# Decode attention at the DMA limit: wo rows as one packet a partition, 112 V tokens in column groups, and the last V piece cut by partitions

## The chip, the cores and the metric

The kernel runs on one core of a Trainium2 chip. The metric is device time in microseconds (us); lower is better. The span is the stretch that the profile covers, from the first to the last instruction; it is about 2 us shorter than the time.

## The reference, cut to what matters

```python
# D = 448; 16 query heads, 8 KV heads (two query heads each), 65,536 keys, head size 256, bf16
q = (x @ wq) ...                                  # one token
scores = einsum("bhqd,bhkd->bhqk", q, k) * 256**-0.5
o = einsum("bhqk,bhkd->bhqd", softmax(scores), v)
a = o.reshape(1, 1, 16 * 256) @ wo                # wo: 4096 x 448
b = ...                                           # a small token mixer, hidden behind the loads
return g * a + (1 - g) * b                        # g: sigmoid gate
```

One token attends to 65,536 keys in each of 8 KV heads. K and V are 268 MB each and are read once. A "pair" below is one KV head with its two query heads. DVE is VectorE, HBM the memory from which K, V and wo are read (544.22 MB by the page). A packet is one entry of the trace's DMA records, here mostly one partition's run (65,536 bytes, 128 tokens, in a whole block); a piece has landed when the trace records the last completion on its semaphore.

## The kernel before

K and V come in 32 blocks of 8 MB each: partition p holds 128 tokens of a block, 512 bytes a token. TensorE transposes K through PSUM, forms scores, and accumulates values. The last block's V is cut into pieces so that little work is left when its last byte lands.

```python
NLATE = 96
pieces = [(NLATE, 112), (112, 124), (124, NV)]      # NV = 128 tokens a partition

# SyncE, one DMA queue; for each block j: K, then V, then wo at the start of a pair
load(vbuf, A_v_cache, j, 0, NLATE if last else NV, 0, sem_v)
if last:
    for (n0, n1), sem in zip(pieces, sem_vp):
        load(vbuf, A_v_cache, j, n0, n1, 0, sem)
if j % PPH == 0:
    ...
    eng.dma_start(wo_sb[:, :, :],                   # two runs of 1,792 bytes a partition
                  A_wo[g * REP * DH:(g + 1) * REP * DH, :].rearrange(
                      "(h p j) n -> p h (j n)", h=REP, j=2)).then_inc(sem_wo, 16)
...
# TensorE: values of a block; token n uses column group n % 4
pe.matmul(acc[o:o + REP, 0:DH], pT[:, r, 2 * nt:2 * nt + 2], vbuf[:, n, :], ...)

def by_d(dst):                                      # the "turn": sum the column groups, put d on partitions
    for dj in range(2):
        ins = pe.matmul(dst[:, dj * REP:(dj + 1) * REP], accs[:, dj:DH:2], sel[:, :], start=False, ...)

def tail():                                         # last block only
    late_values(*pieces[0])                         # V as stationary operand, d on partitions at once
    pe.wait_ge(s_cp, H)                             # DVE has copied the accumulators
    by_d(sps[:, 0, 0:2 * REP])
    late_values(pieces[1][0], NV).then_inc(s_late, 1)
    pe.wait_ge(sem_wo, 16 * H); pe.wait_ge(s_oTn, H)
    project()
# ... (cut)
```

The softmax here doesn't subtract the row's maximum and nothing guards it: scores larger than these inputs give would overflow.

Of the kernel before, what the change touches and what calls it, by code (L numbers as in the profile page):

```python
# [12 lines left out]
def bass_gated_mix__gqa_block_cached__mixer_token_mlp__decode_kernel(  # L13
# [22 lines left out]
    REP = HQ // H  # L36
# [24 lines left out]



    NLATE = 96
    pieces = [(NLATE, 112), (112, 124), (124, NV)]


    NCG = 4
# [22 lines left out]
    with ctx:  # L91
        def sb(shape, dt, name):
            return ctx.enter_context(nc.sbuf_tensor(name, shape, dt))
# [17 lines left out]

        wo_sb = sb([P, REP, 2 * DM], bf16, "wo_sb")

        early = vbuf[:, :, :].rearrange("p n d -> p (n d)")
        early_f = vbuf_f[:, :, :].rearrange("p n d -> p (n d)")
        wq_a = early[:, 0:WF * NQ].rearrange("p (j n) -> p j n", j=WF)
# [26 lines left out]
        zrow = sb([1, NACC], bf16, "zrow")  # L143
        rden = sb([P, REP], f32, "rden")
        densum = sb([P, REP], f32, "densum")
        b2_b = sb([1, 1], bf16, "b2_b")
        stat = sb([1, 8], f32, "stat")
        statb = sb([1, 8], bf16, "statb")
# [65 lines left out]
        @block.sync  # L214
        def _(eng):
            eng.dma_start(wq_a.rearrange("p j n -> p (j n)"),  # L216
                          A_wq[0:WF * P, :].rearrange("(p j) n -> p (j n)", p=P)).then_inc(sem_wq, 16)
            eng.dma_start(wq_b, A_wq[WF * P:DM, :].rearrange("r (a n) -> (r a) n", a=2)  # L218
                          ).then_inc(sem_wq, 16)
            def load(dst, cache, j, n0, n1, at, sem):  # L220
                eng.dma_start(dst[:, at + n0:at + n1, :].rearrange("p n d -> p (n d)"), src(cache, j, n0, n1)  # L221
                              ).then_inc(sem, 16)

            for j in range(NP):
                last = j == NP - 1
                if j >= 1:
                    eng.wait_ge(sem_tr[NB - 1], BODY * (j - 1) + DC)
                if j == 0:
                    load(kring, A_k_cache, j, HV, NV, 0, sem_k)
                    load(kring, A_k_cache, j, 0, HV, 0, sem_kb)  # L230
                elif last:
                    load(kring, A_k_cache, j, 0, HV, HV, sem_k)
                    load(kring, A_k_cache, j, HV, NV, HV, sem_kb)
                else:
                    load(kring, A_k_cache, j, 0, NV, HV * (j % 2), sem_k)
                if j == 0:
                    eng.wait_ge(s_q, 1)
                    eng.wait_ge(s_hb, 1)
                else:
                    eng.wait_ge(sem_pv, j)  # L240
                load(vbuf, A_v_cache, j, 0, NLATE if last else NV, 0, sem_v)
                if last:
                    for (n0, n1), sem in zip(pieces, sem_vp):
                        load(vbuf, A_v_cache, j, n0, n1, 0, sem)
                if j % PPH == 0:
                    g = j // PPH
                    if g >= 1:
                        eng.wait_ge(s_proj, g)
                    eng.dma_start(wo_sb[:, :, :],
                                  A_wo[g * REP * DH:(g + 1) * REP * DH, :].rearrange(  # L250
                                      "(h p j) n -> p h (j n)", h=REP, j=2)).then_inc(sem_wo, 16)
            eng.wait_ge(s_fin, 1)
            eng.dma_start(out_ap, out_g[0:P:P // NCG, :]).then_inc(sem_out, 16)
            eng.wait_ge(sem_out, 16)
# [13 lines left out]
        def _(pe):  # L268
# [54 lines left out]
            def values(j, c0, u16):  # L323
                with pe.If(j == NP - 1):
                    spin(8)
                pe.wait_ge(sem_exp, c0 + (BODY + 2))
                for r in range(BODY):
                    pe.matmul(acc[:, DENC:SELC], ones_sq[:, :], pT[:, r, :],  # L328
                              start=False, stop=(r == BODY - 1), skip_group_check=True)

                def some(n0, n1):
                    pe.wait_ge(sem_v, u16)
                    for n in range(n0, n1):
                        r, nt = divmod(n, NT)
                        o = 32 * (n % 4)
                        ins = pe.matmul(acc[o:o + REP, 0:DH], pT[:, r, 2 * nt:2 * nt + 2], vbuf[:, n, :],  # L336
                                        start=False, stop=False, skip_group_check=True)
                    return ins

                some(0, NLATE).then_inc(s_early, 1)  # L340
                with pe.If(j < NP - 1):
                    some(NLATE, NV).then_inc(sem_pv, 1)
                with pe.Else():
                    tail()

            def piece_wait(n):
                for (n0, _), sem in zip(pieces, sem_vp):
                    if n == n0:
                        pe.wait_ge(sem, 16)

            def late_values(n0, n1):
                for n in range(n0, n1):
                    r, nt = divmod(n, NT)
                    piece_wait(n)
                    for dj in range(2):
                        ins = pe.matmul(sps[:, 0, dj * REP:(dj + 1) * REP], vbuf[:, n, dj:DH:2],  # L356
                                        pT[:, r, 2 * nt:2 * nt + 2], start=(n == NLATE and dj == 0),
                                        stop=(n == NV - 1), skip_group_check=True)
                return ins

            def by_d(dst):
                for dj in range(2):
                    ins = pe.matmul(dst[:, dj * REP:(dj + 1) * REP], accs[:, dj:DH:2], sel[:, :],
                                    start=False, stop=True, skip_group_check=True)
                return ins

            def clear(bank):
                pe.matmul(bank, ones_sq[0:1, :], zrow[0:1, 0:bank.shape[-1]], start=True, stop=True,
                          skip_group_check=True)

            def project():
                for hh in range(REP):
                    for dj in range(2):
                        j = dj * REP + hh
                        for q in range(NCG):
                            ins = pe.matmul(prj[32 * q:32 * q + 1, 0:WG], oTn[:, j:j + 1],  # L376
                                            wo_sb[:, hh, dj * DM + q * WG:dj * DM + (q + 1) * WG],
                                            start=False, stop=True, skip_group_check=True)
                ins.then_inc(s_proj, 1)


            def tail():
                late_values(*pieces[0])
                pe.wait_ge(s_cp, H)
                by_d(sps[:, 0, 0:2 * REP])
                late_values(pieces[1][0], NV).then_inc(s_late, 1)
                pe.wait_ge(sem_wo, 16 * H)
                pe.wait_ge(s_oTn, H)
                project()

            pe.sem_inc(sem_qk, 2)
            pe.wait_ge(sem_ident, 1)
# [34 lines left out]
            with nc.Fori(0, H, 1, engines=on, head_slot={pe.engine: 0}) as g:  # L427
                with nc.Fori(0, PPH, 1, engines=on, head_slot={pe.engine: 0}) as m:
                    j = pe.snap(g * PPH + m, min_val=0, max_val=NP - 1)
                    c0 = pe.snap(j * BODY, min_val=0, max_val=NC)  # L430
                    u16 = pe.snap(j * 16 + 16, min_val=16, max_val=16 * NP)
                    keys(c0, j, u16, pe.snap(x2_reg, min_val=0, max_val=NV))
                    values(j, c0, u16)
                    with pe.If(j < FT):
                        pe.wait_ge(s_pb, j + 1)
                        for q in range(NCG):
                            pe.matmul(prj[32 * q:32 * q + 1, WG:2 * WG], w2cur[:, :],
                                      gu[:, q * WG:(q + 1) * WG], start=False, stop=True, skip_group_check=True)
                    pe.reg_sub(x2_reg, NV, x2_reg)
                with pe.If(g < H - 1):  # L440
                    pe.wait_ge(s_cp, g + 1)
                    clear(acc[:, 0:NACC])
                    by_d(acc[:, SELC:NACC]).then_inc(s_sel, 1)
                    pe.wait_ge(sem_wo, pe.snap(g * 16 + 16, min_val=16, max_val=16 * H))
                    pe.wait_ge(s_oTn, g + 1)
                    project()

        @block.vector
        def _(vec):
# [107 lines left out]
            def finish_head(g):  # L557
                take(vec.snap(g * PPH + PPH, min_val=PPH, max_val=NP))
                vec.tensor_copy(qcur[:, :, :], qT[:, :, bass.ds(g * REP + REP, REP)])
                vec.drain()  # L560
                vec.wait_ge(s_sel, g + 1)
                by_head(acc[:, SELC:NACC])

            vec.wait_ge(s_q, 1)
            vec.tensor_copy(qT[:, :, :].rearrange("p a b -> p (a b)"), sps[:, 1, 0:2 * HQ])
# [23 lines left out]
            with nc.Fori(NC - NCPH, NC, BODY, engines=on) as c0:  # L589
                for k in range(BODY):  # L590
                    evacuate(k, c0 + k)
            take(NP, s_early)
            vec.wait_ge(s_late, 1)
            by_head(sps[:, 0, 0:2 * REP])
            vec.wait_ge(s_proj, H)
# [71 lines left out]
```

## Time and profile before

| | before |
|---|---|
| time, median | 1267.58 us in the first three runs, 1267.51 of six |
| span of the profiled run | 1265.7 us |
| DMA queue of K, V, wo | 99.6% of 16 engines' span |
| TensorE matmul busy | 72% |
| last landings of successive K blocks | 38.70 us apart; 39.91 us with a wo load between |

From the page of the kernel before, parts 1 to 3: the busy time of TensorE with its share of the span, the DMA row of 40 slices in tenths, packet counts, and the main queue (packets, MB, share of 16 engines).

```profile
PE 911.9 (72%) x17040; PEld 861.1 (68%) x17041; DVE 418.2 (33%) x741; ACT 537.2 (42%) x786; POOL 0.9 (0%) x7
...
DMA  9999999999999999999999999999999999999998
...
DMA packets 12509, 544.39 MB, mean 430 GB/s; under 512 B 1360, under 2 KB 3410, under 8 KB 3794
...
q1 hardware_dynamic: 12408, 544.22, 99.6%
```

The DMA row is nine in every slice but the last, and the queue share leaves nothing: the kernel is as long as its loads plus a start and a tail. The packets under 2 KB matter for the change: 2,048 of them are the wo rows.

The timeline of the tail before (start us, us, engine, line, operation, shapes, count, idle before it and what ended it):

```profile
1257.11 2.79 PE L336 MATMUL acc<-vbuf,pT 128*2 128x256 bf16 x96 [0.72 <-DMA vbuf<-in_A_v_cache_dram]
1259.83 0.96 PE L356 MATMUL sps<-pT,vbuf 128*128 128x2 bf16 x32
1259.95 0.46 DVE L543 COPY accs<-acc 128x288 f32<-128x288 f32 x1 [6.80 <-PE acc L336]
...
1260.65 0.61 PE L363 MATMUL sps<-sel,accs 128*128 128x2 f32 x4
...
1261.45 0.95 PE L356 MATMUL sps<-pT,vbuf 128*128 128x2 bf16 x32 [0.19 <-DMA vbuf<-in_A_v_cache_dram]
1262.44 0.16 DVE L554 TENSOR_TENSOR oTn<-sps,rden 128x4 bf16<-128x4 f32 x1 [1.51 <-PE sps L356]
...
1262.75 0.54 PE L376 MATMUL prj<-wo_sb,oTn 128*1 128x112 bf16 x16 [0.35 <-DVE oTn L554]
...
1263.70 0.65 SPq L253 DMA_DIRECT2D out_dram<-out_g  x1
```

The turn (L363) is finished, at 1261.26 us, when the piece of tokens 112 to 124 lands (1261.40). The wait of the second L356 group is for DMA, so that landing, and not TensorE, is what the end of the kernel hangs on.

### The profile page before, as it was taken

The page shows a single profiled execution, that of the slowest core. Times are in us where ns is not written, and L with a number is a line of the kernel's source. Part 1 is how long each engine was busy: PE and PEld are TensorE (multiplying, and loading weights), DVE is VectorE, ACT ScalarE, POOL GpSimd, SP SyncE. Part 2 cuts the span into 40 slices and gives each one's busy share as a digit, 9 for nine tenths or more (in the row PEclk, how much of TensorE's full clock was granted, in tenths as well). Part 3 has the DMA queues.
Part 4 walks back from the last instruction along what each step waited for, and adds up shares of the span by engine and source line. Part 5 has one row for each costly group of instructions (what it writes and reads, how often), then busy time and mean ns, then how long its engine had stood idle before and what let it go on. Part 6 is the DMA issues. An engine that isn't in the chain of part 4 may idle for free.

```text
span 1265.7 us, 38663 instructions
## 1 busy us (share of the span) xinstructions
PE 911.9 (72%) x17040; PEld 861.1 (68%) x17041; DVE 418.2 (33%) x741; ACT 537.2 (42%) x786; POOL 0.9 (0%) x7
## 2 busy tenths in 40 slices
PE   2876668766778666787666876768867678666698
PEld 2766668766677666686665876657766578665687
DVE  2433334333344233343222332223322233331233
ACT  1543335533355333454333553335543245432455
POOL 0000000000000000000000000000000000000000
PEclk9888789788898788888788888789887788887989
DMA  9999999999999999999999999999999999999998
GB/s 412 428 429 437 431 435 433 433 431 437 431 433 435 431 433 437 429 435 435 431 433 433 433 435 435 431 427 439 433 435 435 425 433 439 433 435 429 431 426 353
DMA packets 12509, 544.39 MB, mean 430 GB/s; under 512 B 1360, under 2 KB 3410, under 8 KB 3794
## 3 DMA queue, kind: packets, MB, share of 16 engines
q1 hardware_dynamic: 12408, 544.22, 99.6%
q8 instruction: 8, 0.13, 0.0%
q10 hardware_dynamic: 90, 0.01, 0.0%
q14 instruction: 3, 0.02, 0.0%
HBM read 544.22 MB, written 0.00 MB: 430 GB/s over the span
## 4 chain that ended last, share of the span: by engine, by line
DMA 70%; PE 29%; issue 1%; SPq 0%; DVE 0%; ACT 0%; ACTq 0%
DMA kring<-in_A_k_cache_dram 68%; PE kst L284 24%; PE sps L304 4%; DMA vbuf<-in_A_v_cache_dram 2%; PE acc L336 0%; PE sps L356 0%; SPq L221 0%; PE prj L376 0%; SPq L218 0%; SPq L216 0%; PE acc L328 0%; DVE out_g L596 0%; ACT pT L621 0%; DVE oTn L554 0%; ACTq L621 0%
## 5 line engine op out<-in xcount | busy, mean ns | idle before, releaser
L284 PE MATMUL kst<-ident,kring 128*128 128x128 f32 x4096 | 560.9, 298 | 313.2 <-DMA kring<-in_A_k_cache_dram 301.1
L632 ACT ACTIVATE ktT<-kst 128x1024 bf16<-128x1024 bf16 x512 | 499.4, 1021 | 669.1 <-PE kst L284 668.8
L284 PEld LDWEIGHTS kst<-ident,kring 128*128 128x128 f32 x4096 | 511.1, 155 | 322.9 <-issue 320.7
L538 DVE COPY ktT<-kst 128x1024 bf16<-128x1024 bf16 x512 | 354.3, 692 | 771.5 <-PE kst L284 748.2
L304 PEld LDWEIGHTS sps<-qcur,ktT 128*128 128x128 bf16 x8192 | 237.7, 96 | 4.9 <-issue 2.4
L304 PE MATMUL sps<-qcur,ktT 128*128 128x2 bf16 x8192 | 236.7, 163 | 2.0 <-issue 2.0
L336 PE MATMUL acc<-vbuf,pT 128*2 128x256 bf16 x4064 | 145.1, 312 | 2.3 <-issue 1.6
L336 PEld LDWEIGHTS acc<-vbuf,pT 128*2 128x2 bf16 x4064 | 107.3, 95 | 31.6 <-issue 2.1
L621 ACT ACTIVATE pT<-sps 128x32 f32 x256 | 52.2, 204 | 17.0 <-PE sps L304 17.0
L328 PE MATMUL acc<-pT,ones_sq 128*128 128x32 bf16 x256 | 11.7, 178 | 12.2 <-ACT pT L621 12.2
L328 PEld LDWEIGHTS acc<-pT,ones_sq 128*128 128x128 bf16 x256 | 8.6, 96 | 15.2 <-ACT pT L621 14.9
L543 DVE COPY accs<-acc 128x288 f32<-128x288 f32 x8 | 3.7, 458 | 39.6 <-PE acc L336 39.6
L638 ACT ACTIVATE z_b<-z_b 128x448 bf16<-128x448 bf16 x14 | 8.1, 576 | 20.5 <-DVE z_b L525 20.5
L400 PE MATMUL acc<-vbuf 42*128 42x42 bf16 x1 | 0.2, 214 | 8.3 <-DMA b_b<-in_B_b_dram 8.3
L517 DVE TENSOR_TENSOR wtmp<-u_b 128x448 bf16<-128x448 bf16 x14 | 5.5, 393 | 1.0
L523 DVE TENSOR_TENSOR z_b<-u_b,wtmp 128x448 bf16<-128x448 bf16 x14 | 5.5, 393 | 1.0
L519 DVE TENSOR_TENSOR z_b<-wtmp,u_b 128x448 bf16<-128x448 bf16 x14 | 5.5, 393 | 1.0
L531 DVE TENSOR_TENSOR gu<-wtmp,z_b 128x448 bf16<-128x448 bf16 x14 | 5.5, 393 | 1.0
L400 PEld LDWEIGHTS acc<-vbuf 42*128 42x128 bf16 x1 | 0.1, 98 | 8.4 <-DMA b_b<-in_B_b_dram 8.4
L529 DVE TENSOR_SCALAR z_b<-z_b 128x448 bf16<-128x448 bf16 x14 | 3.9, 277 | 5.7 <-ACT z_b L638 5.7
L515 DVE TENSOR_SCALAR u_b<-wtmp,params 128x448 bf16<-128x448 bf16 x14 | 4.7, 337 | 2.6 <-issue 2.6
L513 DVE TENSOR_SCALAR wtmp<-hbT,params 128x448 bf16<-128x448 bf16 x14 | 4.7, 336 | 2.6 <-issue 2.6
(84 smaller groups left out, 76.2 us busy)
## 6 DMA issues: line engine op xcount, KB each, us to landing
kring<-in_A_k_cache_dram SPq DMA_DIRECT2D x4, 4096.0 KB, 24.3
vbuf<-in_A_v_cache_dram SPq DMA_DIRECT2D x1, 6144.0 KB, 24.3
wo_sb<-in_A_wo_dram SPq DMA_DIRECT2D x8, 448.0 KB, 28.6
vbuf<-in_A_wq_dram SPq DMA_DIRECT2D x1, 3072.0 KB, 10.4
vbuf<-in_A_v_cache_dram SPq DMA_DIRECT2D x1, 1024.0 KB, 26.0
vbuf<-in_A_v_cache_dram SPq DMA_DIRECT2D x1, 768.0 KB, 27.5
vbuf<-in_A_wq_dram SPq DMA_DIRECT2D x1, 512.0 KB, 11.2
vbuf<-in_A_v_cache_dram SPq DMA_DIRECT2D x31, 29.8
```

What stands on the lines that cost most here:

```text
L284: ins = pe.transpose(kst[:, b, i * P:(i + 1) * P], kring_f[:, at + NT * (k % DC) + 4 * b + i, :], ident[:, :])
L304: ins = pe.matmul(sps[:, par, 2 * nt:2 * nt + 2], ktT[:, par, b, ntl * DH + dj:(ntl + 1) * DH:2], qcur[:, dj, :], start=(dj == 0), stop=(d ...
L328: pe.matmul(acc[:, DENC:SELC], ones_sq[:, :], pT[:, r, :], start=False, stop=(r == BODY - 1), skip_group_check=True)
L336: ins = pe.matmul(acc[o:o + REP, 0:DH], pT[:, r, 2 * nt:2 * nt + 2], vbuf[:, n, :], start=False, stop=False, skip_group_check=True)
L517: vec.tensor_tensor(W, U, U, op=ALU.mult)
L519: vec.tensor_tensor(Z, W, U, op=ALU.mult)
L523: vec.tensor_tensor(Z, U, W, op=ALU.add)
L531: vec.tensor_tensor(gu[:, :], W, Z, op=ALU.mult).then_inc(s_pb, 1)
L538: vec.tensor_copy(ktT[:, k % KTB, b, :], kst_b[:, b, :]).then_inc(sem_ev[b], 1)
L621: act.activation(pT[:, bass.ds(p0 + k % DC, 1), :].rearrange("p o n -> p (o n)"), sps[:, k % 2, 0:2 * NT], AF.Exp, scale=scale).then_inc(s ...
L632: act.activation(ktT[:, k % KTB, b, :], kst_b[:, b, :], AF.Copy).then_inc(sem_ev[b], 1)
L638: act.activation(z_b[:, :], z_b[:, :], AF.Tanh).then_inc(s_tanh, 1)
```

## The change

The author wanted three things. The wo rows of pairs 0 to 6 should come as one run of 3,584 bytes a partition, half as many packets (the layout then needs another turn, by rows). Sixteen more tokens of the last V block should go through the cheap column groups (2.79 us for 96 tokens in the timeline above, against 0.96 us for 16 late ones). And the last V piece should go as DMAs of 120 and 8 partitions. A filler matmul was put after the late values. The diff, cut to its core:

```diff
-    NLATE = 96
-    pieces = [(NLATE, 112), (112, 124), (124, NV)]
+    NFIRST = 96
+    NLATE = 112
+    pieces = [(NFIRST, NLATE), (NLATE, 124), (124, NV)]
+    by_eight = ((0, 120), (120, P))
...
+        rrow = sb([P, 1], f32, "rrow")
...
+            def load(dst, cache, j, n0, n1, at, sem, parts=((0, P),)):
+                for p0, p1 in parts:
+                    eng.dma_start(dst[p0:p1, at + n0:at + n1, :]..., src(cache, j, n0, n1)[p0:p1, :]).then_inc(sem, 16)
...
-                        load(vbuf, A_v_cache, j, n0, n1, 0, sem)
+                        load(vbuf, A_v_cache, j, n0, n1, 0, sem, by_eight if n1 == NV else ((0, P),))
...
+                    if g < H - 1:
+                        eng.dma_start(wo_rows, w.rearrange("(p i) n -> p (i n)", i=2 * REP)).then_inc(sem_wo, 16)
...
-                some(0, NLATE).then_inc(s_early, 1)
+                some(0, NFIRST)
...
+                    some(NFIRST, NLATE, last=True).then_inc(s_early, 1)
...
+            def by_row(dst):
+                for hh in range(REP):
+                    for i in range(2 * REP):
+                        ins = pe.matmul(dst[hh * HP:(hh + 1) * HP, i:i + 1], accs[:, i:DH:2 * REP], sel[:, hh:hh + 1], ...)
...
             def tail():
-                late_values(*pieces[0])
                 pe.wait_ge(s_cp, H)
                 by_d(sps[:, 0, 0:2 * REP])
-                late_values(pieces[1][0], NV).then_inc(s_late, 1)
+                late_values(NLATE, NV).then_inc(s_late, 1)
+                spin(1)
...
+                for hh in range(REP):                       # DVE, at the end of pairs 0 to 6
+                    h = slice(hh * HP, (hh + 1) * HP)
+                    vec.tensor_copy(rrow[h, :], rden[h, hh:hh + 1])
+                vec.drain()
                 vec.wait_ge(s_sel, g + 1)
-                by_head(acc[:, SELC:NACC])
+                vec.tensor_scalar(oTn[:, :], acc[:, SELC:NACC], rrow[:, :], None, op0=ALU.mult).then_inc(s_oTn, 1)
```

More of the change, by code (lines that the diff above doesn't have):

```diff
@@ L112, in bass_gated_mix__gqa_block_cached__mixer_token_mlp__decode_kernel @@
         wo_sb = sb([P, REP, 2 * DM], bf16, "wo_sb")
+        wo_rows = wo_sb[:, :, :].rearrange("p h n -> p (h n)")
+        HP = P // REP
+        assert 2 * REP * HP == DH
         early = vbuf[:, :, :].rearrange("p n d -> p (n d)")
@@ L219, in _ @@
                           ).then_inc(sem_wq, 16)
-            def load(dst, cache, j, n0, n1, at, sem):
-                eng.dma_start(dst[:, at + n0:at + n1, :].rearrange("p n d -> p (n d)"), src(cache, j, n0, n1)
-                              ).then_inc(sem, 16)
+            def load(dst, cache, j, n0, n1, at, sem, parts=((0, P),)):
+                for p0, p1 in parts:
+                    eng.dma_start(dst[p0:p1, at + n0:at + n1, :].rearrange("p n d -> p (n d)"),
+                                  src(cache, j, n0, n1)[p0:p1, :]).then_inc(sem, 16)
             for j in range(NP):
@@ L240, in _ @@
                     eng.wait_ge(sem_pv, j)
-                load(vbuf, A_v_cache, j, 0, NLATE if last else NV, 0, sem_v)
+                load(vbuf, A_v_cache, j, 0, NFIRST if last else NV, 0, sem_v)
                 if last:
                     for (n0, n1), sem in zip(pieces, sem_vp):
-                        load(vbuf, A_v_cache, j, n0, n1, 0, sem)
+                        load(vbuf, A_v_cache, j, n0, n1, 0, sem, by_eight if n1 == NV else ((0, P),))
                 if j % PPH == 0:
@@ L248, in _ @@
                         eng.wait_ge(s_proj, g)
-                    eng.dma_start(wo_sb[:, :, :],
-                                  A_wo[g * REP * DH:(g + 1) * REP * DH, :].rearrange(
-                                      "(h p j) n -> p h (j n)", h=REP, j=2)).then_inc(sem_wo, 16)
+                    w = A_wo[g * REP * DH:(g + 1) * REP * DH, :]
+                    if g < H - 1:
+                        eng.dma_start(wo_rows, w.rearrange("(p i) n -> p (i n)", i=2 * REP)).then_inc(sem_wo, 16)
+                    else:
+                        eng.dma_start(wo_sb[:, :, :], w.rearrange("(h p j) n -> p h (j n)", h=REP, j=2)
+                                      ).then_inc(sem_wo, 16)
             eng.wait_ge(s_fin, 1)
@@ L329, in values, with some @@
                               start=False, stop=(r == BODY - 1), skip_group_check=True)
-                def some(n0, n1):
-                    pe.wait_ge(sem_v, u16)
+                def some(n0, n1, last=False):
+                    if last:
+                        piece_wait(n0)
+                    else:
+                        pe.wait_ge(sem_v, u16)
                     for n in range(n0, n1):
@@ L338, in some @@
                     return ins
-                some(0, NLATE).then_inc(s_early, 1)
+                some(0, NFIRST)
                 with pe.If(j < NP - 1):
-                    some(NLATE, NV).then_inc(sem_pv, 1)
+                    some(NFIRST, NV).then_inc(sem_pv, 1)
                 with pe.Else():
+                    some(NFIRST, NLATE, last=True).then_inc(s_early, 1)
                     tail()
             def piece_wait(n):
-                for (n0, _), sem in zip(pieces, sem_vp):
+                for (n0, n1), sem in zip(pieces, sem_vp):
                     if n == n0:
-                        pe.wait_ge(sem, 16)
+                        pe.wait_ge(sem, 16 * len(by_eight) if n1 == NV else 16)
             def late_values(n0, n1):
@@ L356, in late_values @@
                         ins = pe.matmul(sps[:, 0, dj * REP:(dj + 1) * REP], vbuf[:, n, dj:DH:2],
-                                        pT[:, r, 2 * nt:2 * nt + 2], start=(n == NLATE and dj == 0),
+                                        pT[:, r, 2 * nt:2 * nt + 2], start=False,
                                         stop=(n == NV - 1), skip_group_check=True)
@@ L363, in by_d @@
                     ins = pe.matmul(dst[:, dj * REP:(dj + 1) * REP], accs[:, dj:DH:2], sel[:, :],
-                                    start=False, stop=True, skip_group_check=True)
+                                    start=(dj == 0), stop=True, skip_group_check=True)
+                return ins
+            def by_row(dst):
+                for hh in range(REP):
+                    for i in range(2 * REP):
+                        ins = pe.matmul(dst[hh * HP:(hh + 1) * HP, i:i + 1], accs[:, i:DH:2 * REP],
+                                        sel[:, hh:hh + 1], start=False, stop=True, skip_group_check=True)
                 return ins
@@ L369, in clear, with project @@
                           skip_group_check=True)
-            def project():
-                for hh in range(REP):
-                    for dj in range(2):
-                        j = dj * REP + hh
-                        for q in range(NCG):
-                            ins = pe.matmul(prj[32 * q:32 * q + 1, 0:WG], oTn[:, j:j + 1],
-                                            wo_sb[:, hh, dj * DM + q * WG:dj * DM + (q + 1) * WG],
-                                            start=False, stop=True, skip_group_check=True)
+            def project(cols):
+                for i, j in enumerate(cols):
+                    for q in range(NCG):
+                        ins = pe.matmul(prj[32 * q:32 * q + 1, 0:WG], oTn[:, j:j + 1],
+                                        wo_rows[:, i * DM + q * WG:i * DM + (q + 1) * WG],
+                                        start=False, stop=True, skip_group_check=True)
                 ins.then_inc(s_proj, 1)
             def tail():
-                late_values(*pieces[0])
                 pe.wait_ge(s_cp, H)
                 by_d(sps[:, 0, 0:2 * REP])
-                late_values(pieces[1][0], NV).then_inc(s_late, 1)
+                late_values(NLATE, NV).then_inc(s_late, 1)
+                spin(1)
                 pe.wait_ge(sem_wo, 16 * H)
                 pe.wait_ge(s_oTn, H)
-                project()
+                project([dj * REP + hh for hh in range(REP) for dj in range(2)])
             pe.sem_inc(sem_qk, 2)
@@ L442, in _ @@
                     clear(acc[:, 0:NACC])
-                    by_d(acc[:, SELC:NACC]).then_inc(s_sel, 1)
+                    by_row(acc[:, SELC:NACC]).then_inc(s_sel, 1)
                     pe.wait_ge(sem_wo, pe.snap(g * 16 + 16, min_val=16, max_val=16 * H))
                     pe.wait_ge(s_oTn, g + 1)
-                    project()
+                    project(range(2 * REP))
         @block.vector
@@ L591, in _ @@
                     evacuate(k, c0 + k)
-            take(NP, s_early)
+            take(1, s_early)
             vec.wait_ge(s_late, 1)
```

## The prediction

The sum: 1267.58 - 0.50 + 0.05 comes to 1267.13 us.

> **What bounds it now.** DMA. By the page's queue line, the queue that carries K, V and wo takes 99.6% of 16 engines' span; the DMA row of the slices is all nines but one. In the table of groups the transposes sat idle 301 us for K. In the trace's packet records, the last landings of successive K blocks are 38.70 us apart, and 39.91 us with a wo load between: a wo load costs 1.20 us of the stream. At the rate of the 64 KB packets (2.42 us each) its 28,672 bytes an engine would take 1.06 us, so 0.14 us is the price of 16 small packets. Packets of 2,048 and 4,096 bytes (0.084 and 0.159 us) give 36.6 ns per 1,000 bytes and 9 ns fixed.[...]
>
> **What the change does.**
> 1. wo of seven pairs: 128 packets of 3,584 bytes for 256 of 1,792, 8 fewer an engine and pair. 8 x 9 ns x 7 = 0.50 us of DMA time saved. The queue never runs dry, so all of it should shorten the span.
> 2. Between pairs: 8 float32 matmuls for 2 (the old loads took 0.14 us each; estimate +1.7 us a pair) and two tiny copies on DVE (about 0.3 us). PE then waits some 10 us for K, and loads are issued many us ahead. Cost: nothing.
> 3. The tail. By the timeline before, 96 V tokens run in column groups from 1257.11 (26 ns each), 16 late tokens from 1259.83 (0.87 us of loads), then the turn by the selector until 1261.2; the second-to-last piece lands at 1261.40, then 32 matmuls (0.95 us), DVE, projection, output. With 112 tokens in column groups, the last ends near 1260.3, the copy of the accumulators (0.46 us) near 1260.8, the turn (0.61 us) near 1261.45: just when the piece lands. The end stays within 0.1 us, if anything 0.05 us later.
> 4. The last piece as 120 and 8 partitions: [...] The last piece lands at 1262.00, while the 24 matmuls ahead of it (0.70 us) run until 1262.14: worth nothing on the chain.
> 5. One filler matmul while PE waits 0.3 us for DVE: nothing, or 0.05 us either way.
>
> **Sum.** 1267.58 - 0.50 + 0.05 = about 1267.1 us. Range 1266.4 to 1267.6 us (8 in 10). Chances: faster by over 2% 0.005, within 2% 0.99, slower by over 2% 0.005.
>
> **What would show it.** Step 1: 1,792-byte packets of one pair only; 3,584-byte packets near 0.140 us; K landings 39.84 us apart across a wo load, 38.70 elsewhere. Step 2: intervals without wo unchanged; PE's idle time for K shrinks by the added work. Step 3: from the landing of the last large V load (96 tokens, 1257.07) to the end of the span 8.6 us as before, within 0.1. Step 4: the last late matmuls do not wait for DMA.
>
> **What would make it wrong.** A packet cost above the fit; a turn by rows that delays the issue of loads; the selector's turn limiting the tail by more than 0.1 us; a difference of chip or day above the half microsecond at stake.

## The result, and the profile after

The changed kernel took 1268.28 us (median of six runs, 1267.85 to 1268.38) against 1267.51 us (1267.39 to 1267.93). The ratio is the mean time of one kernel's runs over that of the other's of the same rounds, so not quite the ratio of the medians: 1.0005, with a 95% interval of 0.9992 to 1.0018. The prediction said 1267.1 and at most 1267.6: a gain of half a microsecond became a loss of 0.8. The interval of the ratio alone can't settle differences this small. The trace can.

The same parts of the page after:

```profile
PE 921.3 (73%) x17110; PEld 867.5 (69%) x17110; DVE 420.6 (33%) x755; ACT 536.7 (42%) x786; POOL 0.9 (0%) x7
...
DMA packets 11620, 544.39 MB, mean 430 GB/s; under 512 B 1367, under 2 KB 1625, under 8 KB 2905
...
q1 hardware_dynamic: 11519, 544.22, 99.5%
```

Some 890 packets fewer, as intended: 896 of 3,584 bytes replace 1,792 of 1,792. K landings across a wo load of those pairs are 39.83 us apart in place of 39.91, and 38.70 elsewhere, as predicted. The last large V load (96 tokens) lands at 1256.66 us, 0.41 us earlier than before. So the gain exists, up to this point. The tail's timeline after:

```profile
1256.70 3.23 PE L354 MATMUL acc<-vbuf,pT 128*2 128x256 bf16 x112 [0.73 <-DMA vbuf<-in_A_v_cache_dram]
1259.98 0.46 DVE L568 COPY accs<-acc 128x288 f32<-128x288 f32 x1 [7.24 <-PE acc L354]
...
1260.49 0.63 PE L382 MATMUL sps<-sel,accs 128*128 128x2 f32 x4 [0.57 <-DVE accs L568]
...
1261.80 1.04 PE L375 MATMUL sps<-pT,vbuf 128*128 128x2 bf16 x32 [0.68 <-DMA vbuf<-in_A_v_cache_dram]
...
1262.88 0.16 DVE L579 TENSOR_TENSOR oTn<-sps,rden 128x4 bf16<-128x4 f32 x1 [1.93 <-PE sps L375]
...
1264.15 0.62 SPq L268 DMA_DIRECT2D out_dram<-out_g  x1
```

TensorE starts 0.41 us earlier (1256.70 against 1257.11), and the turn ends at 1261.12, also early. Then it stands idle for 0.68 us and waits for DMA where it waited 0.19 us before. The late values start 0.35 us later than before. The piece of tokens 112 to 124, whose own DMA was not changed, lands 5.10 us after the large V load in place of 4.34.

Here are the trace's packet records of the pieces (a packet is one partition's run):

```
piece (bytes a packet)        before: min / median / max us    after: min / median / max us
tokens 112 to 124  (6,144)    0.234 / 0.236 / 0.246            0.234 / 0.239 / 0.380
tokens 124 to 128  (2,048)    0.084 / 0.084 / 0.088            0.084 / 0.094 / 0.233
```

The first 2,048-byte packets start at 1258.42 us, while packets of the piece ahead are in flight (the last of those ends at 1261.11 us); from 1258.90 us on, 36 of the 128 packets of 6,144 bytes take longer than 0.246 us, the longest of the kernel before. The windows view of 1258.9 to 1260.9 us (after the busy times: granted clock, DMA busy share, GB/s), first before, then after:

```profile
1258.90:1260.90 2.00, 2.00 (x75) 1.69 (x63) 0.78 (x3) 0.00 (x0) 0.00 (x0) 1.00 0.74 298
```

```profile
1258.90:1260.90 2.00, 1.43 (x44) 1.05 (x32) 0.76 (x3) 0.00 (x0) 0.00 (x0) 1.00 0.71 215
```

The engines are busy almost as long (0.74 and 0.71) but move 215 GB/s in place of 298. Divided by the share that is 403 GB/s of busy engines before and 303 after: busy engines move less.

A second, smaller thing showed in the list of runs. Time minus span was 2.17 us on average after, but 1.80 us in the kernel before. So 0.37 us of the loss is not inside the profiled span at all.

### The profile page after: what moved, and what is told of

It is laid out like the page before. It is cut to its first block, busy times and chain, and to the rows that moved or that the text cites. A ratio compares the mean times of both kernels' runs of the same rounds, so it can differ in the third digit from the quotient of the medians.

```text
span 1266.2 us, 38824 instructions
## 1 busy us (share of the span) xinstructions
PE 921.3 (73%) x17110; PEld 867.5 (69%) x17110; DVE 420.6 (33%) x755; ACT 536.7 (42%) x786; POOL 0.9 (0%) x7
## 4 chain that ended last, share of the span: by engine, by line
DMA 71%; PE 28%; issue 1%; SPq 0%; DVE 0%; ACT 0%; ACTq 0%
DMA kring<-in_A_k_cache_dram 68%; PE kst L299 24%; PE sps L319 4%; DMA vbuf<-in_A_v_cache_dram 2%; PE acc L354 0%; PE sps L375 0%; SPq L233 0%; PE prj L401 0%; SPq L227 0%; SPq L229 0%; PE acc L343 0%; DVE out_g L625 0%; PE kst L335 0%; ACT pT L650 0%; ACTq L650 0%
## 5 line engine op out<-in xcount | busy, mean ns | idle before, releaser
L354 PE MATMUL acc<-vbuf,pT 128*2 128x256 bf16 x4080 | 150.5, 319 | 2.8 <-issue 2.0
L354 PEld LDWEIGHTS acc<-vbuf,pT 128*2 128x2 bf16 x4080 | 110.5, 97 | 34.3 <-issue 2.5
L390 PEld LDWEIGHTS acc<-sel,accs 128*64 128x64 f32 x112 | 10.8, 214 | 0.9
L390 PE MATMUL acc<-sel,accs 128*64 128x1 f32 x112 | 11.4, 260 | 0.0
```

The lines of the kernel that those rows point to most:

```text
L354: ins = pe.matmul(acc[o:o + REP, 0:DH], pT[:, r, 2 * nt:2 * nt + 2], vbuf[:, n, :], start=False, stop=False, skip_group_check=True)
L390: ins = pe.matmul(dst[hh * HP:(hh + 1) * HP, i:i + 1], accs[:, i:DH:2 * REP], sel[:, hh:hh + 1], start=False, stop=True, skip_group_check= ...
```

## The experiments

### Which part costs it

Theory 1: the DMAs of 120 and 8 partitions slow the packets in flight beside them. Rival: the split is innocent, and the column groups or the new order of the tail delay it. Four kernels, five runs each, on one chip, beside nine runs of the kernel before.

`a_whole`: the changed kernel, last piece whole.

```diff
-    by_eight = ((0, 120), (120, P))
+    by_eight = ((0, P),)
```

> The changed kernel with its last V piece in one DMA of 128 partitions again; all else of the change kept. Theory 1[...]: the 6,144-byte packets are again all 0.234 to 0.246 us (they went up to 0.380 with the split), the piece of tokens 112 to 124 lands 4.3 us after the 96-token load as before (5.1 with the split), the span is about 0.9 us shorter than the changed kernel's 1266.2, and the time about 1267.2 to 1267.4. Rival (the split is innocent; the column groups or the second selector turn delay the tail): landing still about 5.1 us after, time still about 1268.2.

`b_split`: the kernel before with only the split.

```diff
+    by_eight = ((0, 120), (120, P))
...                                                              # load() with parts, as above
-                        load(vbuf, A_v_cache, j, n0, n1, 0, sem)
+                        load(vbuf, A_v_cache, j, n0, n1, 0, sem, by_eight if n1 == NV else ((0, P),))
-                        pe.wait_ge(sem, 16)
+                        pe.wait_ge(sem, 16 * len(by_eight) if n1 == NV else 16)
```

> The kernel before with only the last V piece as 120 and 8 partitions. Theory 1: packets of 6,144 bytes stretch to about 0.38 us, the piece of tokens 112 to 124 lands about 5.1 us after the 96-token load in place of 4.33, and the time is 0.7 to 0.9 us above that of before. Rival (innocent split): time of before within 0.15 us.

`b_wo`: the kernel before with only the hunks of wo (the DMA by rows, `by_row`, the order of the projection, the copies on DVE).

```diff
-                    eng.dma_start(wo_sb[:, :, :], ... "(h p j) n -> p h (j n)" ...)
+                    if g < H - 1:
+                        eng.dma_start(wo_rows, w.rearrange("(p i) n -> p (i n)", i=2 * REP)).then_inc(sem_wo, 16)
+                    else: ...                                   # as before
-                    by_d(acc[:, SELC:NACC]).then_inc(s_sel, 1)
+                    by_row(acc[:, SELC:NACC]).then_inc(s_sel, 1)
...                                                              # and the hunk of DVE shown above
```

> The kernel before with only the wo rows of pairs 0 to 6 (one 3,584-byte packet a partition, the turn by rows). Both theories: the landings of K blocks across a wo load 39.83 us apart in place of 39.91, the 96-token load about 0.5 us earlier than in before, time 0.4 to 0.5 us under that of before. If the time outside the span grows with this part (the changed kernel showed 2.15 us between span and time, before 1.85), the gain in time is 0.2 us less.

`b_cols`: the kernel before with only the hunks of `NFIRST` and `NLATE` (112 tokens in column groups, the turn first in its bank).

```diff
+    NFIRST = 96
-    NLATE = 96
+    NLATE = 112
...
-                some(0, NLATE).then_inc(s_early, 1)
+                some(0, NFIRST)
...
+                    some(NFIRST, NLATE, last=True).then_inc(s_early, 1)
...
-                late_values(*pieces[0])
```

> The kernel before with only tokens 96 to 112 moved to column groups (selector turn first in the bank). Theory 1: within 0.1 us of before, since the turn ends before the next piece lands. Rival (this part delays the tail): the late matmuls start after the landing of their piece by 0.3 us or more, and the time is 0.3 to 0.8 us above before.

Medians and means of five runs (nine for before), and from the profiled run the landing of piece 112 to 124 after the large V load:

| kernel | time, median | mean span | time minus span | piece 112 to 124 lands after |
|---|---|---|---|---|
| before | 1267.40 | 1265.63 | 1.80 | 4.34 us |
| after (six runs, earlier) | 1268.28 | 1266.05 | 2.17 | 5.10 us |
| a_whole | 1267.31 | 1265.10 | 2.16 | 4.35 us |
| b_split | 1268.25 | 1266.50 | 1.80 | 5.20 us |
| b_wo | 1267.33 | 1265.22 | 2.14 | 4.35 us |
| b_cols | 1267.30 | 1265.52 | 1.79 | 4.36 us |

In `b_split` TensorE waits 1.05 us for the piece:

```profile
1262.04 0.99 PE L358 MATMUL sps<-pT,vbuf 128*128 128x2 bf16 x32 [1.05 <-DMA vbuf<-in_A_v_cache_dram]
```

Its 6,144-byte packets reach 0.435 us; in the other three all stay within 0.246 us. By the 2% rule all four kernels are "same", with intervals that include 1, but the five times of `b_split` (1268.20 to 1268.57) lie above all nine of before (1267.27 to 1267.75). The rival falls. The parts add up: in span, wo gives -0.41, the column groups -0.11, the split +0.87, in sum +0.35; the changed kernel, from its earlier six runs, has +0.42. Outside the span only the wo part adds, 0.34 us. Together these make the 0.8 us.

Stretched packets are not the whole of it. Counted from the landing of the large V load, the last 6,144-byte packet ends 0.66 us later in the changed kernel than in before, of the 0.76 us by which the piece lands later; in `b_split` it is 0.46 of 0.86 us. The rest lies between the end of the last packet and the last completion that the trace records, and is not explained.

Small parts of the sum carry a noise that repeats don't remove. The second K block lands at 72.7 to 73.0 us, depending on the kernel. And in the profiled runs of before, the changed kernel and `b_split` the granted TensorE clock fell from 1.0 to 0.5 before or while the last projection ran: 0.54 us for its 16 matmuls, against 0.37 us in `a_whole`, `b_wo` and `b_cols`. Edits that execute nothing new (`b_alloc` and `b_pad` below) show 0.37 us too, so the 0.17 us is not the work of a part. From the landing of the large V load to the end, `b_cols` takes 8.53 us, `b_alloc` and `b_pad` with the old tail at the same clock 8.54 and 8.55 us: the column groups gain nothing. The wo part is better read between landings (below), and the split keeps its size at equal clock: 9.58 us in `b_split` against 8.68 in before.

`a_whole` brings the span down by 0.95 us against the changed kernel, up to 0.17 of which can be the clock. Its tail, with the last piece whole:

```profile
1260.16 0.63 PE L382 MATMUL sps<-sel,accs 128*128 128x2 f32 x4 [0.57 <-DVE accs L568]
...
1260.72 0.98 PE L375 MATMUL sps<-pT,vbuf 128*128 128x2 bf16 x32
...
1262.04 0.37 PE L401 MATMUL prj<-wo_sb,oTn 128*1 128x112 bf16 x16 [0.35 <-DVE oTn L579]
```

The late values follow the turn with no DMA wait: the turn ends within about 0.1 us of the piece's landing (1260.67), as the prediction had it for this part.

### Why the split is slow

The last piece is only 256 KB. To measure the shape by itself, I loaded a whole V block (8 MB, block 16, in mid-run) in other cuts. In the kernel before, that load lands at 676.48 us.

`mid_120_8`: 120 and 8 partitions. The text names two outcomes, packets that keep their 2.42 us and packets that don't. The 4.8, 9.7 and 40 to 50 us of the second are my estimate, two and four times 2.42 us, and no run had shown those factors.

```diff
+                if j == 16:
+                    for p0, p1, sem in ((0, 120, sem_mid), (120, P, sem_v)):
+                        eng.dma_start(vbuf[p0:p1, :, :]..., src(A_v_cache, j)[p0:p1, :]).then_inc(sem, 16)
+                else:
                     load(vbuf, A_v_cache, j, 0, NLATE if last else NV, 0, sem_v)
...
+                with pe.If(j == 16):
+                    pe.wait_ge(sem_mid, 16)
```

> The kernel before, but the V load of block 16 (8 MB of 16.8, middle of the run) goes as a DMA of 120 partitions and one of 8. In before that V load lands 19.37 us after its K load. [...]it lands 19.4 + 2.4 = 21.8 us after, and all 64 KB packets stay at 2.42 us. [...]packets take about 4.8 us in the first DMA, up to 9.7 us in the second, and the load lands 40 to 50 us after; the span grows by some 20 to 30 us.

`mid_tokens`: two DMAs as well, but cut by tokens.

```diff
+                    load(vbuf, A_v_cache, j, 0, NV // 2, 0, sem_mid)
+                    load(vbuf, A_v_cache, j, NV // 2, NV, 0, sem_v)
```

> Control: the same V load of block 16 as two DMAs too, but each of 128 partitions and half the tokens (32 KB packets). Both theories of the engines: 19.4 us after K, packets of 1.21 us, span as before within 0.3 us. If two DMAs in place of one were the trouble, it would be longer.

`mid_112_16` and `mid_64_64`: as `mid_120_8` with the cut at 112 and at 64.

```diff
-                    for p0, p1, sem in ((0, 120, sem_mid), (120, P, sem_v)):
+                    for p0, p1, sem in ((0, 112, sem_mid), (112, P, sem_v)):      # or 64
```

> The kernel before with the V load of block 16 as DMAs of 112 and 16 partitions[...].[...] If every DMA that isn't of 128 partitions runs at half speed: 39 us or more.[...] (a small model of the 16 engines, an estimate from the 2.42 us packet): 112 partitions need 23 to 26 us, both together about 30 us; the model gives 41 and 49 to 51 us for 120 and 8, where about 47 and 54 were measured.

> The same V load as two DMAs of 64 partitions[...]. [...]about 41 us after K, nearly all packets near 5.1 us. By the rival that collisions come only with uneven shapes: 19.4 us.

The windows view of 660 to 672 us, in the middle of these loads (same columns as above), for the kernel before, `mid_tokens`, `mid_120_8`, `mid_112_16` and `mid_64_64`, in that order:

```profile
660.00:672.00 12.00, 12.00 (x200) 11.94 (x199) 6.23 (x9) 9.19 (x13) 0.00 (x0) 0.92 1.01 437
```

```profile
660.00:672.00 12.00, 12.00 (x199) 11.94 (x198) 6.21 (x9) 9.10 (x13) 0.00 (x0) 0.92 1.01 434
```

```profile
660.00:672.00 12.00, 12.00 (x171) 11.91 (x170) 6.12 (x9) 8.20 (x12) 0.00 (x0) 0.88 0.93 191
```

```profile
660.00:672.00 12.00, 12.00 (x171) 11.91 (x170) 5.99 (x9) 8.07 (x12) 0.00 (x0) 0.88 0.91 218
```

```profile
660.00:672.00 12.00, 12.00 (x174) 11.87 (x173) 6.36 (x10) 8.55 (x12) 0.00 (x0) 0.91 0.96 197
```

A DMA share of 0.9 or more looks like a queue that does its best, yet only 191 to 218 GB/s move, less than half. Busy engines are not fast engines.

| kernel | V of block 16 lands | span | packets of 64 KB |
|---|---|---|---|
| before | 676.48 us | 1265.7 | 2.42 us |
| mid_tokens | 676.47 us | 1265.8 | (32 KB) 1.22 us |
| mid_120_8 | 711.92 us | 1301.1 | 5.1 us, then 9.4 to 11.2 us while the 8 load |
| mid_112_16 | 701.17 us | 1290.1 | mostly 2.7 to 5.0 us, then up to 9.8 us |
| mid_64_64 | 699.14 us | 1288.1 | 5.1 us |

Two DMAs in place of one cost nothing (`mid_tokens`). A cut by partitions costs 22 to 35 us for one load of 8 MB, and the span grows by just as much. So the first outcome of `mid_120_8` (21.8 us after K expected) falls, and so does "only uneven shapes": 64 and 64 is even and slow. The second outcome, my estimate, was too mild for `mid_120_8`: it expected the landing 40 to 50 us after K and a span longer by 20 to 30 us; from K's normal landing (657.1 us) it was 54.8 us, and the span grew by 35.4 us.

What the runs show is rates. With 64 partitions a DMA it is 197 GB/s and packets of 5.1 us, a little over twice 2.42. While the DMA of 8 partitions loads, packets take 9.4 to 11.2 us, about four times 2.42. No run shows the mechanism; a packet record names no engine. The 41 us expected of `mid_64_64` came close (42 us from K's normal landing), but it was an estimate.

`mid_112_16` was predicted badly. My small model's estimate was about 30 us for both DMAs; from K's normal landing to 701.17 us it was 44 us. The rival "half speed for anything but 128 partitions" came closer there, but does not explain packets of 8 to 9.8 us, nor those of 2.7 to 3.5 us in its middle. Why its packets differ so much stays open.

### Receiving side or sending side

In all these runs the partition number fixes the source row as well: rows lie 64 KB apart in HBM, and so 2 MB from a row to the 32nd after it. Two more kernels change the distance in the source. The texts give two outcomes each, the first for a cause on the receiving side, the second for a cause in the source; the 2 MB were my choice, and no run had pointed to them. Both load other tokens' values on purpose. (The comparison with the reference still passed: one block in 32 of a softmax this flat changes the output too little. That check alone would not have found such a bug.)

```diff
+ # src_64_64: 64 + 64 partitions, source rows 128 KB apart instead of 64 KB
+ far = gv[0:P * 2 * NV, :].rearrange("(p n) d -> p n d", p=P)[:, 0:NV, :].rearrange("p n d -> p (n d)")
+ # src_128: 128 partitions, twice 64 tokens, source rows 32 KB apart
+ near = gv[a * P * NV // 2:(a + 1) * P * NV // 2, :].rearrange("(p n) d -> p (n d)", p=P)
```

> As mid_64_64 (V load of block 16 as two DMAs of 64 partitions), but the source rows are 128 KB apart in place of 64 KB[...] (wrong result on purpose: the values belong to other tokens). [...]packets near 5.1 us, about 205 GB/s, V lands 42 us after K as in mid_64_64. If the source's distance of 2 MB collided: 2.42 us, 19.4 us after K.

> The V load of block 16 as two DMAs of 128 partitions by 64 tokens, each from 4 MB of rows 32 KB apart, so that partitions p and p+64 read 2 MB apart[...] (wrong result on purpose). [...]full speed, 32 KB packets of 1.21 us, 19.4 us after K. If the source's distance collided: packets near 2.5 us and about 40 us.

The windows view of 660 to 672 us, `src_64_64` first, then `src_128`:

```profile
660.00:672.00 12.00, 12.00 (x170) 11.95 (x169) 6.03 (x9) 8.20 (x12) 0.00 (x0) 0.86 0.98 202
```

```profile
660.00:672.00 12.00, 12.00 (x202) 11.94 (x201) 6.23 (x9) 9.38 (x14) 0.00 (x0) 0.94 1.00 431
```

V lands at 699.22 us (699.14 in `mid_64_64`) and at 676.51 us. With the source rows moved, 64 partitions stay slow (202 GB/s); with 128 partitions, rows 2 MB apart are read at full speed (431 GB/s). So it is not this distance in the source that decides; the slowness goes with the partitions that one DMA writes. Whether it is their number or which ones they are was not tested apart, and the mechanism was not shown.

### The time outside the span

The wo part adds 0.34 us that no view of the profile shows. Candidates: the DMA's form, the longer program of TensorE, the copies on DVE, or the new tile that moves others in memory.

`b_rows2`: the wo part, but each row fetched as two DMAs of 1,792 bytes a partition.

```diff
-                        eng.dma_start(wo_rows, w.rearrange("(p i) n -> p (i n)", i=2 * REP)).then_inc(sem_wo, 16)
+                        wv = w.rearrange("(p i) n -> p (i n)", ...).rearrange("p (a m) -> p a m", a=2)
+                        eng.dma_start(wo_sb[:, 0:1, :]..., wv[:, 0:1, :]...).then_inc(sem_wh, 16)
+                        eng.dma_start(wo_sb[:, 1:2, :]..., wv[:, 1:2, :]...).then_inc(sem_wo, 16)
```

> The wo part with its turn by rows, projection order and DVE copies, but each wo row of 3,584 bytes fetched as two DMAs of 1,792 bytes a partition. If the packet count is what saves: landings of K across a wo load 39.91 to 39.93 us apart again, span as before. If the code of the turn by rows (or its copies) is what adds 0.35 us outside the span: time minus span 2.15 again, so the time is about 0.35 us above before. If the DMA's form is what adds it: 1.80.

`b_pad`: before, with the 8 matmuls of the turn by rows behind a branch that is never taken.

```diff
+                with pe.If(pe.snap(x2_reg, min_val=0, max_val=NV) == 1):     # x2_reg is 0 or 128
+                    by_row(acc[:, SELC:NACC])
```

> The kernel before plus the 8 matmuls of the turn by rows behind a branch that is never taken. If the size of PE's program causes the 0.35 us outside the span: time minus span about 2.15. If not: 1.80, and time as before.

`b_dve`: before, with only the two copies on DVE, their tile and the drain.

```diff
+                for hh in range(REP):
+                    h = slice(hh * 64, (hh + 1) * 64)
+                    vec.tensor_copy(rrow[h, :], rden[h, hh:hh + 1])
+                vec.drain()
```

> The kernel before plus only the two tiny DVE copies (and one drain) of the change at each pair's end; their result is not used. If the extra 0.35 us outside the span come from DVE's longer program: time minus span about 2.15. If from PE's executed turn by rows: 1.80 and time as before.

`b_alloc`: the tile `rrow` alone. `b_dve_never`: tile, copies and drain behind a branch that is never taken. `b_dve_full`: two executed copies of 128 partitions into a dead tile, with the drain and without the new tile.

```diff
+ # b_alloc and b_dve_never
+        rrow = sb([P, 1], f32, "rrow")
+ # b_dve_never: the lines of b_dve under
+                with vec.If(vec.snap(kt_reg, ...) == FT + 5):                # kt_reg is at most FT
+ # b_dve_full
+                for hh in range(REP):
+                    vec.tensor_copy(densum[:, hh:hh + 1], rden[:, hh:hh + 1])
+                vec.drain()
```

> The kernel before plus only the allocation of the small tile rrow (4 bytes a partition), never used; all tiles allocated after it move by 4 bytes. If placement in memory makes the 0.35 us outside the span: time minus span 2.15. If not: 1.80 and time as before.

> The kernel before plus the tile and the two copies and their drain behind a branch of DVE that is never taken. If the length of DVE's program makes the 0.35 us: time minus span 2.15. If the copies must be executed: 1.80, unless b_alloc shows 2.15 as well.

> The kernel before plus two executed tiny DVE copies of all 128 partitions into a dead tile and one drain, no new tile. If execution or program length makes the 0.35 us: 2.15. If the placement does: 1.80.

| kernel (4 runs each) | time, median | before beside it | mean span | time minus span |
|---|---|---|---|---|
| b_rows2 | 1267.69 | 1267.50 | 1265.50 | 2.19 |
| b_pad | 1267.52 | 1267.50 | 1265.80 | 1.77 |
| b_dve | 1267.96 | 1267.52 | 1265.83 | 2.16 |
| b_alloc | 1267.44 | 1267.44 | 1265.67 | 1.78 |
| b_dve_never | 1267.44 | 1267.44 | 1265.62 | 1.81 |
| b_dve_full | 1267.79 | 1267.44 | 1265.65 | 2.17 |

The six kernels that execute such copies (the changed one, `a_whole`, `b_wo`, `b_rows2`, `b_dve` and `b_dve_full`) have 2.14 to 2.19; all the others have 1.74 to 1.85, single runs included. The DMA's form, placement and program length fall: it takes executing the copies with the drain that follows them. The six always have both, so the copies are not separated from the drain. The group of them in `b_dve` (line, operation, count; busy us, mean ns; idle before):

```profile
L564 DVE COPY rrow<-rden 64x1 f32<-64x1 f32 x14 | 2.1, 148 | 0.6
```

They run between 180 and 1117 us, long before the end, and are 2 us of work on an engine that is idle two thirds of the time. Why they show in time outside the span is not found. The cost is shown, the mechanism is open. `b_rows2` also confirms the packet count as the source of the gain: with 1,792-byte packets again its K landings across a wo load are 39.91 us apart. From the second K landing to the large V load it takes 1184.11 us (before 1184.09), the changed kernel 1183.66 and `b_wo` 1183.70. Its mean span nevertheless lies 0.23 us under that of before beside it, so a difference of means of that size shows nothing here.

### A version that beats both

`best` keeps the wo rows and the column groups, loads all pieces with 128 partitions, scales by two multiplies of 64 partitions in place of the copies, and cuts the last 16 tokens into 8, 6 and 2.

```diff
-    pieces = [(NFIRST, NLATE), (NLATE, 124), (124, NV)]
-    by_eight = ((0, 120), (120, P))
+    pieces = [(NFIRST, NLATE), (NLATE, 120), (120, 126), (126, NV)]
+    by_eight = ((0, P),)
...
-                    vec.tensor_copy(rrow[h, :], rden[h, hh:hh + 1])
-                vec.drain()
-                vec.wait_ge(s_sel, g + 1)
-                vec.tensor_scalar(oTn[:, :], acc[:, SELC:NACC], rrow[:, :], None, op0=ALU.mult).then_inc(s_oTn, 1)
+                    ins = vec.tensor_scalar(oTn[h, :], acc[h, SELC:NACC], rden[h, hh:hh + 1], None, op0=ALU.mult)
+                ins.then_inc(s_oTn, 1)
```

> A version meant to beat both: wo rows and 112 column-group tokens of the change, no split by partitions, the pair's scaling as two DVE multiplies of 64 partitions in place of two copies, a drain and one multiply, and the last 16 tokens as pieces of 8, 6 and 2 in place of 12 and 4. The 96-token load to the end: 8.55 us with whole pieces; the smaller last pieces should take 0.1 to 0.2 us off it. Span about 1264.9 (a_whole 1265.1); time 1266.7 if the outside share falls back to 1.80, 1267.1 if it stays at 2.15.

It took 1266.82 us (1266.59 to 1266.87, five runs) against 1267.52 us of before on the same chip (1267.30 to 1267.61, nine runs): no overlap, 0.70 us. Ratio 0.9995, interval 0.9981 to 1.0008. Mean span 1265.00, and time minus span is back at 1.78. The pieces of 8, 6 and 2 gave much less than the 0.1 to 0.2 us expected: from the large V load to the end `best` takes 8.51 us, `a_whole` 8.54. Of the gain over before, the wo packets explain about 0.4 us; the rest is no more than the noise of start and clock. That time minus span is back at 1.78 with 14 multiplies in place of 7 shows that more DVE instructions alone don't cost it; `best` has neither the copies nor their drain.

## Why the prediction was wrong

1. wo packets: right. It said 8 packets fewer an engine and pair at 9 ns each, 0.50 us in all. K intervals shrank by 0.075 us at six of the seven loads, 0.45 us (the first load falls into the start, where intervals vary), and the stretch from the second K landing to the large V load by 0.43 us. The packets took 0.144 us where the fit gave 0.140; that cost nothing that the intervals show.
2. "Between pairs: ... Cost: nothing." Right for the span: intervals without wo stayed at 38.70 us, and TensorE's idle time for K fell from 301 to 293 us as its work grew. Wrong for the time: the "two tiny copies on DVE (about 0.3 us)" cost, with their drain, 0.34 us outside the span, which I had not thought to look at.
3. The tail: right. The turn ends at 1261.12 us, 4.46 us after the large V load, where 1261.45 (4.38 after) had been predicted; when the last piece is whole it does not delay the late values. The check that was named for this step, 8.6 us from the large V load to the end within 0.1, failed in the changed kernel (9.55 us), but by the split: `a_whole` has 8.54 us and `b_cols` 8.53.
4. The last piece: "worth nothing on the chain." This is the step that failed, worth 0.87 us in `b_split`. I counted packets, and asked only when the last piece would land. I did not ask whether packets of the piece ahead, still in flight, would be slowed by it. They were: up to 0.380 us in place of 0.246, and that piece is the one the chain hangs on. The check named for this step looked at the wrong piece and nearly held: the last eight matmuls start at 1262.49 us, 0.05 us after the last piece lands. The changed kernel's trace has 23 completions of the last piece at its landing, where the kernel before has 16.
5. The filler matmul: as predicted, no cost seen. DVE's product to the projection's first weight load is 0.28 us both before and after.

Nothing that I had listed under what would make it wrong explains the loss. That the split could slow packets in flight was not on the list.

## What to carry to other kernels

In a saturated stream like this one, keep every DMA on 128 partitions, and cut a load by its free dimension when you need a smaller last piece: the cut by tokens was free (434 GB/s against 437), the cut by partitions brought the rate of the whole queue down to 191 to 218 GB/s while it ran, and stretched packets of the DMA ahead too (up to 0.380 us in place of 0.246). Read the busy share of DMA engines together with GB/s, because here engines counted as busy over 0.9 moved less than half. And compare time minus span between two kernels: a difference there, 0.35 us, is a cost that no view of the profile showed.
